# Channel attention with a SwiGLU stage on one core: low parts of split operands change engines, two differences become one, steps of the schedule move

## Chip, cores and metric

The kernel runs on one core of a Trainium2 chip. The metric is the device time of one execution in microseconds (us). Engines are called by their names: TensorE (PE in the profile; PEld is its weight load), VectorE (DVE), ScalarE (ACT), GpSimd (POOL), and SyncE (SP), whose queue issues most DMAs.

## The reference

```python
# attention over channels, per batch (B = 2, N = 6016 rows, C = 256 channels)
qn = q / (norm(q, axis=1) + 1e-6);  kn = k / (norm(k, axis=1) + 1e-6)
s = kn.transpose(0, 2, 1) @ qn / tau          # 256 x 256
a = softmax(s, axis=-1)
x = (v @ a).reshape(B * N, C)                 # 12032 x 256
# SwiGLU (d_ff = 1536)
xn = x / sqrt(mean(x * x, axis=-1) + 1e-6) * rms_g
g = xn @ w_gate;  val = xn @ w_val
out = (g * sigmoid(g) * val) @ w_out          # 12032 x 256
```

All is float32, and the output has 12032 rows of 256.

## The kernel before, in words

**Split operands.** Every matmul operand is kept as two fp32r tiles, a high part (the value rounded, made by ScalarE with a copy) and a low part (value minus high part, a subtraction). A product is three matmuls: high x high, high x low, low x high. Where the low parts are made, on VectorE or on GpSimd, is what much of the change is about.

**Blocks and steps.** The rows are worked on in 24 blocks of up to 512 rows (4 tiles of 128; the first of batch 0 and the last of batch 1 have 3). A block has 12 steps, f = 0 to 11, one for each 128 of the 1536 columns of w_gate and w_val. Blocks 0, 1 and 23 use plain products (`emit_hidden`). Blocks 2 to 22 use `emit_step`: seven products of half size in place of eight, for gate (even f) or value (odd f) of a pair p = f // 2. A step works on three flights at once: it starts f (products 5 and 1, into a PSUM tile pu of three buffers), continues f - 1 (3 and 6) and ends f - 2 (7, 2 and 4). ScalarE copies partial sums from PSUM into t (L810, L815), VectorE adds them to what comes later (L803, L804) into zg (gate) or zv (value). For a gate ScalarE applies SiLU (L819, L837); for a value VectorE multiplies it into zg (L822, and L831 for the quarter that product 4 ends). TensorE can't issue product 4 of a step before L803 has read its PSUM tile, nor use a tile again before L831 or L837 has. zg has two buffers, t two, zv one.

**Rounding and turned pairs.** After a pair's odd step `round_pair` lists its splits: gx (at the end of that step, `run_rounds` on ScalarE, then `run_subs` for the low part), gy and gz "later" (start of the next odd step). In blocks 4 to 22 the pairs 1 to 4 are turned: their output uses seven products too. gx is made of three quarters of zg (128x768). Then, in the middle of the next even step, `run_turned` overwrites the quarters of zg by differences, on VectorE, four of 128x256 (L728); gy (quarters 0 and 3) and gz (1 and 2) are split from these, the low parts on GpSimd (L742). As the low part of gx reads zg, the differences wait for it. In pairs 0 and 5 gx and gy have two quarters each (128x512) and nothing is overwritten. The output matmuls of f (L998) come five steps after f; a pair's first listed uses are of high parts.

**Order by hand.** The order on every engine is the order of emission. For blocks from 5 on, tables `steady_mid` (emitted in the middle of a step, after SiLU and differences or the product, ahead of the output matmuls) and `steady` (at the end of a step) say which step of the neighbouring blocks' work goes where. j is the block of the step:

- vm(0), v1: VectorE transposes (L427) of halves of v of block j + 3 or j + 2 into vw (one buffer); vh0, vh1: their high parts (ScalarE, L443); vl0, vl1: low parts (L448); x0, x1: px = v x a on TensorE (L459); q, r, n: squares (ScalarE, L475), reciprocal root (GpSimd, L484 and L488) and scaling (ScalarE, L500), into the tile "xn" of one buffer.
- m0, m1: VectorE transposes (L539) of the normalised rows of block j + 2 into a tile "moved" of one buffer; m1 also issues 16 DMAs of 32 KB on SP's queue (L548), which bring the turned rows into "xn".
- scale: ScalarE (L558) for block j + 1; parts: three GpSimd differences of xn's quarters (L570, L575), into "moved"; xh0, xh1 and xl0, xl1: high (L601) and low parts (L614) of the two rounds of xt of block j + 1, each round two operations (128x256 and 128x512; two of 128x512).
- copy, sums_, c0, c1 (VectorE, L1023, L1032): the output sums of block j - 1; store: two VectorE transposes (L1043) and four DMAs of 128 KB; load: four DMAs of 128 KB of v for block j + 3, into the buffer that store used.

In blocks 0 to 3 other tables hold; block 4 has `turn4` and `turn4_mid`, which override some entries. Before, vl0, vl1, xl0 and xl1 of the blocks from 4 on are on VectorE; xl1 is emitted in two parts (xl1a, xl1b).

Of the kernel before, what the change touches and what calls it, by code (L numbers as in the profile page):

```python
# [12 lines left out]
ALU = mybir.AluOpType  # L13
# [6 lines left out]
def kernel(  # L20
# [17 lines left out]
    nc = tc.nc  # L38
# [54 lines left out]
    def f32(ap):  # L93
        return ap.bitcast(F32)
# [61 lines left out]
    for b, sizes in enumerate(([2] * 2 + [4] * 9 + [2] * 3 + [1], [CH] * 11 + [3])):  # L156
        t = 0
# [174 lines left out]
    for b in range(B):  # L332
        t = 0
        while t < NT:
            n = (NT - t) % BT or BT if b == 0 else min(BT, NT - t)
# [6 lines left out]
    v_t, v_w, vT, xps, xnt, xT, xp, moved = {}, {}, {}, {}, {}, {}, {}, {}  # L342
# [36 lines left out]
    def half_tiles(j, h):  # L379
        return list(range(2 * h, min(2 * h + 2, blocks[j][2])))  # L380
# [61 lines left out]
        new_vT(j, h)  # L442
        nc.scalar.activation(out=vT[j, h][0][:, :, :m], in_=v_w[j, h][:, :, :m], func=AF.Copy)  # L443

    def split_v_low(j, h):
        m = len(half_tiles(j, h)) * P
        vh, vl = (x[:, :, :m] for x in vT[j, h])
        nc.vector.tensor_tensor(out=vl, in0=v_w.pop((j, h))[:, :, :m], in1=f32(vh), op=ALU.subtract)  # L448

    def emit_x(j, h):  # L450
        ah, al = a_hl[blocks[j][0]]
# [125 lines left out]
    def xT_round(j, i):  # L577

        h = blocks[j][2] * P // 2
        slots = ((0, 1), (1, 3)) if i == 0 else ((3, 5), (5, 7))  # L580
        hi, lo = ([y[:, a:b] for a, b in slots] for y in xp[j])
        if i == 0:
            whole = moved[j][0] if isinstance(moved[j], tuple) else moved[j]
            x = [whole[:, c, :2 * h].rearrange("p (i n) -> p i n", i=2) for c in range(KC)]
            src = [x[0][:, :1], x[1]]
        else:
            src = [moved[j][1][:, m:m + 2, :h] for m in (0, 2)]
        return src, hi, lo

    def emit_xT_high(j, i):  # L590
        if i == 0:
            new_xT(j)
        if j == NB - 1:
            if i == 0:
                nc.scalar.activation(
                    out=xT[j][0], in_=moved[j][:, :, :blocks[j][2] * P], func=AF.Copy
                )
            return
        src, hi, _ = xT_round(j, i)
        for o, x in zip(hi, src):  # L600
            nc.scalar.activation(out=o, in_=x, func=AF.Copy)  # L601

    def emit_xT_low(j, i, engine=nc.vector, part=None):
        if j == NB - 1:
            if i == 0:
                nc.vector.tensor_tensor(
                    out=xT[j][1], in0=moved[j][:, :, :blocks[j][2] * P], in1=f32(xT[j][0]),
                    op=ALU.subtract,
                )
            return  # L610
        src, hi, lo = xT_round(j, i)
        for k, (o, x, y) in enumerate(zip(lo, src, hi)):
            if part in (None, k):
                engine.tensor_tensor(out=o, in0=x, in1=f32(y), op=ALU.subtract)  # L614

    def emit_xT_round(j, i):
        emit_xT_high(j, i)
        emit_xT_low(j, i, nc.gpsimd)

# [60 lines left out]
    def so_part(tiles, m):  # L682
        if len(tiles) > 1 and m == 2:
            return tiles[1]
        return tiles[0][:, m * P:(m + 1) * P]
# [4 lines left out]
    rounds, subs, later, turned = [], [], [], []  # L690

    def new_g(tag, n, j, f):
        return [
            g_p.tile([P, n * HN], F32R, tag=f"{tag}{i}", name=f"g{tag}{i}_{j}_{f}") for i in range(2)
        ]

    def by_quarter(t, n, h):
        return t[:, :n * h].rearrange("p (i n) -> p i n", i=n)

    def round_pair(j, p, zg, h):  # L700

        x, y = new_g("x", 3, j, 2 * p), new_g("y", 2, j, 2 * p + 1)
        engine = nc.gpsimd
        w = [[w[:, 2 * p + i, e * P:(e + 1) * P] for w in wo] for i in range(2) for e in range(2)]
        if strassen(j, p):
            z = new_g("z", 2, j, 2 * p + 1)
            a12, a22, a11, s4 = w
            s1, s2, s3 = ([so_part(s[PAIRS.index(p)], m) for s in so_hl] for m in range(3))
            turned.append(zg)
            rounds.append((zg[:, :3], *(by_quarter(t, 3, h) for t in x), engine))  # L710
            later.append((zg[:, 0:4:3], *(by_quarter(t, 2, h) for t in y), engine))
            later.append((zg[:, 1:3], *(by_quarter(t, 2, h) for t in z), engine))
            q = [[t[:, i * h:(i + 1) * h] for t in x] for i in range(3)]
            r = [[t[:, i * h:(i + 1) * h] for t in g] for g in (y, z) for i in range(2)]
            G[j, 2 * p] = [(2, 0, a11, q[0]), (0, 0, a12, q[1]), (0, h, s4, q[2])]
            G[j, 2 * p + 1] = [
                (3, h, s1, r[0]), (3, 0, s3, r[1]), (1, 0, a22, r[2]), (2, h, s2, r[3]),
            ]
        else:
            rounds.append((zg[:, 1:3], *(by_quarter(t, 2, h) for t in x), engine))  # L720
            later.append((zg[:, 0:4:3], *(by_quarter(t, 2, h) for t in y), engine))
            for i, g in enumerate((x, y)):
                G[j, 2 * p + i] = [(e, 0, w[2 * i + e], [t[:, :2 * h] for t in g]) for e in range(2)]

    def run_turned():
        for z in turned:
            for o, i0, i1 in ((0, 3, 0), (3, 2, 3), (2, 2, 0), (1, 1, 2)):
                nc.vector.tensor_tensor(out=z[:, o], in0=z[:, i0], in1=z[:, i1], op=ALU.subtract)  # L728
        turned.clear()

    def strassen(j, p=PAIRS[0]):
        return STRA <= j < NB - 1 and p in PAIRS
# [6 lines left out]

    def run_subs():  # L740
        for hh, gh, gl, engine in subs:
            engine.tensor_tensor(out=gl, in0=hh, in1=f32(gh), op=ALU.subtract)  # L742
        subs.clear()

# [311 lines left out]
    with tc.manual_schedule():  # L1056
# [42 lines left out]
        for i in range(nch):  # L1099
            n = chunks[0][i][1]  # L1100
# [22 lines left out]
        parts = [(i, t, min(2, n - t)) for i, (_, n) in enumerate(chunks[1]) for t in range(0, n, 2)]  # L1123
# [70 lines left out]
        for f in range(NF):  # L1194
# [8 lines left out]
            n = 2 if f % 2 else 1  # L1203
# [31 lines left out]
        for i in (2, 3, 0, 1):  # L1235
            for p in range(NP):
                j, f = divmod(NF + at_step[p][i], NF)
# [8 lines left out]
        for p in range(NP):  # L1246
            j, f = divmod((NB - 2) * NF + 2 * p + 4, NF)
# [37 lines left out]
        def vm(h):  # L1285
            def run(n):
                move_v(n, h)
                if h == 1 and 2 < n + 1 < STRA + 2:
                    load_v(n + 1)
            return run  # L1290

        def vs(h):
            return lambda n: split_v(n, h)
# [13 lines left out]
        def xm(c):  # L1307
            return lambda n: emit_xT_move(n, c)
# [4 lines left out]
        def of(m, go):  # L1313

            def run(j):
                n = j + m
                if m < 0 and n < WINO or n >= NB:
                    return
                go(n)
            return run  # L1320

        v0, s0, v1, s1 = (of(2, go) for go in (vm(0), vs(0), vm(1), vs(1)))
        x0, q0, r0, n0, x1, q1, r1, n1 = (of(2, go(h)) for h in range(2) for go in (x, sq, rr, xn))
        m0, m1 = (of(2, xm(c)) for c in range(KC))
        scale, parts, hi, rest = (of(1, go) for go in (emit_xT_scale, emit_xT_parts, xr(0), xr(1)))
        copy, sums_, c0, c1, store = (of(-1, go) for go in (
            post_copy, post_sums, lambda j: post_out(j, 0), lambda j: post_out(j, 1), post_store,
        ))
        after = lambda m, *gos: tuple(of(m, go) for go in gos)
        load = of(3, load_v)  # L1330

        vh0, vl0, vh1, vl1 = (of(2, lambda n, go=go, h=h: go(n, h)) for h in range(2) for go in (split_v_high, split_v_low))
        xh0, xl0, xh1, xl1 = (of(1, lambda n, go=go, i=i: go(n, i)) for i in range(2) for go in (emit_xT_high, emit_xT_low))

        xl1a, xl1b = (of(1, lambda n, k=k: emit_xT_low(n, 1, part=k)) for k in range(2))

        steady = {
            0: (vl0,),
            1: (xh0, v1),
            2: (copy, sums_),  # L1340
            3: (vh1,),
            4: (c0, c1),
            5: (xh1,),
            7: (xl1b, load),
            8: (m0,),
            10: after(3, vm(0)),
        }
        steady_mid = {
            1: (scale,),
            2: (parts, xl0),  # L1350
            3: (x0, q0, r0),
            4: (vl1, n0),
            5: (x1, q1, r1),
            6: (n1, store),
            7: (xl1a,),
            9: (m1,),
            11: after(3, lambda n: split_v_high(n, 0)),
        }
        turn4 = {
            **steady,  # L1360
            0: (vh0,),
            1: (vl0,),
            2: (),
            3: (xh0, v1),
            4: (vh1, c0, c1),
        }
        turn4_mid = {
            **steady_mid,
# [1 line left out]
            2: (),  # L1370
            3: (scale,),
            4: (lambda j: build_so(2, 2), parts, xl0, x0),
            5: (vl1, q0, r0),
            6: (n0, x1, q1, r1, store),
            8: (n1,),
        }
        turn3 = {
            3: (v0,),
# [54 lines left out]
        for i, (j, f) in enumerate(steps):  # L1433
# [4 lines left out]
            k = min(j, 5)  # L1438
# [68 lines left out]
```

## Time and profile before

| what | value |
|---|---|
| time, median of 3 runs | 1349.29 us (1348.26 to 1349.37) |
| the profiled execution's own time | 1349.69 us |
| its span | 1347.7 us |
| mean granted TensorE clock | 0.996 |
| busy: TensorE / VectorE / ScalarE / GpSimd | 1272.7 / 1037.1 / 854.0 / 646.7 us |

Busy times are sums over the whole span, in which the first 200 us or so (scores, weights, the first two blocks) have other limits than the blocks from 4 to 22. Busy of TensorE includes the filling and draining of its pipeline, so a busy TensorE isn't one at its peak. A row of a timeline has the start in us, the duration (of all instructions of a merged row together), engine, line, operation, tiles and shapes, a count, and in brackets how long the engine stood before it and what ended that.

### The profile page before, as it was taken

How to read it: one execution, taken by the hardware profiler on the slowest of the kernel's cores; microseconds unless marked ns; L12 is line 12 of the kernel's file. 1: busy time of each engine (PE TensorE's matmuls, PEld its weight loads, DVE VectorE, ACT ScalarE, POOL GpSimd, SP SyncE). 2: the span in 40 equal slices, each digit the busy share in tenths (PEclk: the TensorE clock that was granted, in tenths of full speed). 3: DMA queues.
4: the chain of work that ended last, by engine and by line, in shares of the span. 5: the costliest groups of instructions: out<-in, count | busy, mean ns of one | idle time of the engine just before them, and what ended most of it. 6: DMA issues, size and time to landing. Idle time of an engine off the chain costs nothing.

```text
span 1347.7 us, 25377 instructions
## 1 busy us (share of the span) xinstructions
PE 1272.7 (94%) x9312; PEld 1205.9 (89%) x9312; DVE 1037.1 (77%) x1746; ACT 854.0 (63%) x1765; POOL 646.7 (48%) x531
## 2 busy tenths in 40 slices
PE   8999999998999899899999998998999999989998
PEld 7899889998889889898888898998988888989998
DVE  5799698677877877778788778777887887787763
ACT  5666557666666676666666676665666666766652
POOL 0210367465545545455455455455555554555550
PEclk9999999998999999999999999999999999999999
DMA  8966312022020220220211202202112012021021
GB/s 289 322 233 214 96 28 48 16 48 32 17 46 10 41 36 13 48 32 17 48 17 33 41 7 48 35 15 48 26 24 48 16 34 40 9 45 18 19 71 28
DMA packets 229372, 75.97 MB, mean 56 GB/s; under 512 B 186880, under 2 KB 220800, under 8 KB 229248
## 3 DMA queue, kind: packets, MB, share of 16 engines
q1 hardware_dynamic: 228416, 73.12, 22.9%
q8 instruction: 73, 1.20, 0.4%
q10 hardware_dynamic: 832, 1.25, 0.3%
q14 instruction: 51, 0.42, 0.1%
HBM read 48.50 MB, written 14.42 MB: 47 GB/s over the span
## 4 chain that ended last, share of the span: by engine, by line
PE 66%; DVE 15%; POOL 6%; DMA 4%; issue 4%; SPq 2%; ACT 2%; DVEq 0%; ACTq 0%; POOLq 0%
PE pu L774 30%; PE po L998 16%; POOL gx L742 6%; PE px L459 5%; DVE zg L728 4%; PE pq L774 4%; PE pg L891 3%; PE s L185 3%; PE pv L891 3%; PE po L944 3%; DVE zv L803 2%; DMA raw<-in_k_dram 2%; DVE vt L448 2%; SPq L548 2%; DVE xw L539 2%
## 5 line engine op out<-in xcount | busy, mean ns | idle before, releaser
L774 PE MATMUL pu<-xt,w 128*128 128x256 f32 x2268 | 397.6, 284 | 43.8 <-DVE zv L803 40.6
L774 PEld LDWEIGHTS pu<-xt,w 128*128 128x128 f32 x2268 | 326.7, 189 | 64.9 <-DVE zv L803 51.3
L774 PE MATMUL pu<-xt,s 128*128 128x256 f32 x2268 | 362.4, 284 | 18.9 <-DVE zg L831 17.7
L774 PEld LDWEIGHTS pu<-xt,s 128*128 128x128 f32 x2268 | 314.5, 189 | 35.2 <-DVE zg L831 24.7
L742 POOL TENSOR_TENSOR gx<-zg,gx 128x768 fp32r<-128x768 f32 (+1 forms) x126 | 205.6, 1632 | 216.3 <-PE pu L774 131.1
L742 POOL TENSOR_TENSOR gy<-zg,gy 128x512 fp32r<-128x512 f32 x126 | 165.8, 1316 | 227.1 <-ACT gy L736 214.1
L815 ACT ACTIVATE t<-pu 128x512 f32<-128x512 f32 x252 | 150.8, 598 | 147.3 <-DVE zv L804 105.8
L728 DVE TENSOR_TENSOR zg<-zg 128x256 f32<-128x256 f32 x304 | 129.3, 425 | 126.3 <-POOL gx L742 118.5
L998 PE MATMUL po<-gx,w 128*128 128x256 f32 (+1 forms) x984 | 190.0, 314 | 0.0
L822 DVE TENSOR_TENSOR zg<-zg,zv 128x768 f32<-128x768 f32 x126 | 161.7, 1283 | 12.4 <-DVE zv L804 0.9
L736 ACT ACTIVATE gx<-zg 128x768 fp32r<-128x768 f32 (+1 forms) x126 | 95.9, 761 | 113.4 <-DVE zg L831 103.0
L998 PEld LDWEIGHTS po<-gx,w 128*128 128x128 f32 x984 | 140.5, 188 | 4.7
L774 PE MATMUL pq<-xt,w 128*128 128x256 f32 x756 | 130.3, 281 | 0.0
L810 ACT ACTIVATE t<-pu 128x256 f32<-128x256 f32 x252 | 94.5, 375 | 38.8 <-PE pu L774 38.4
L742 POOL TENSOR_TENSOR gz<-zg,gz 128x512 fp32r<-128x512 f32 x76 | 111.5, 1467 | 0.0
L803 DVE TENSOR_TENSOR zg<-pu,t 128x512 f32<-128x512 f32 x126 | 85.3, 677 | 32.4 <-PE pu L774 22.5
L736 ACT ACTIVATE gy<-zg 128x512 fp32r<-128x512 f32 x126 | 80.5, 639 | 46.6 <-DVE zg L728 45.4
L774 PEld LDWEIGHTS pq<-xt,w 128*128 128x128 f32 x756 | 107.4, 190 | 0.0
L819 ACT ACTIVATE zg<-zg 128x768 f32<-128x768 f32 x126 | 105.9, 840 | 0.1
L803 DVE TENSOR_TENSOR zv<-pu,t 128x512 f32<-128x512 f32 x126 | 84.2, 669 | 15.9 <-ACT zg L837 7.6
L185 PE MATMUL s<-raw 128*128 128x256 f32 x376 | 86.2, 382 | 4.1 <-DMA raw<-in_k_dram 4.0
L998 PE MATMUL po<-gy,w 128*128 128x512 f32 x300 | 85.4, 393 | 0.0
(173 smaller groups left out, 2160.9 us busy)
## 6 DMA issues: line engine op xcount, KB each, us to landing
v<-in_v_dram SPq DMA_DIRECT2D x84, 128.0 KB, 3.7
xnT<-xw SPq DMA_DIRECT2D x336, 32.0 KB, 1.9
out_dram<-ob SPq DMA_DIRECT2D x84, 128.0 KB, 3.3
raw<-in_q_dram SPq DMA_DIRECT2D x20, 512.0 KB, 5.5
raw<-in_k_dram SPq DMA_DIRECT2D x19, 512.0 KB, 6.2
wraw<-in_moe_w_gate_dram SPq DMA_DIRECT2D x12, 256.0 KB, 5.7
wraw<-in_moe_w_val_dram SPq DMA_DIRECT2D x12, 256.0 KB, 5.9
wraw<-in_moe_w_out_dram SPq DMA_DIRECT2D x12, 256.0 KB, 5.6
```

The costliest lines, as they stand in the source:

```text
L185: nc.tensor.matmul(out=s_ps[b][:, c, :], lhsT=r[:, 1, t, c * P:(c + 1) * P], rhs=r[:, 0, t, :], start=(t0 + t == 0 and c == 0), stop=(t0 + ...
L728: nc.vector.tensor_tensor(out=z[:, o], in0=z[:, i0], in1=z[:, i1], op=ALU.subtract)
L736: nc.scalar.activation(out=gh, in_=hh, func=AF.Copy)
L742: engine.tensor_tensor(out=gl, in0=hh, in1=f32(gh), op=ALU.subtract)
L774: nc.tensor.matmul(out=out, lhsT=wm[wi], rhs=xm[xi], start=(start and q == 0), stop=(q == 2), skip_group_check=True,)
L803: nc.vector.tensor_tensor(out=z[:, 1:], in0=u, in1=t[:, :2], op=ALU.add)
L810: nc.scalar.activation(out=mt[:, 0], in_=mu[:, 1], func=AF.Copy)
L815: nc.scalar.activation(out=nt[:, 1:], in_=nu, func=AF.Copy)
L819: nc.scalar.activation(out=zg[:, 1:], in_=zg[:, 1:], func=AF.Silu)
L822: nc.vector.tensor_tensor(out=zg[:, 1:], in0=zg[:, 1:], in1=z, op=ALU.mult)
L891: nc.tensor.matmul(out=t[:, :n], lhsT=wgv[wi][:, f, c, wj, :], rhs=x[xi][:, c, :n], start=(m == 0), stop=(m == 3 * KC - 1),)
L998: nc.tensor.matmul(out=acc[b][:, o:o + g.shape[-1]], lhsT=w, rhs=g, start=first, stop=True, skip_group_check=True,)
```

## The change

In turned pairs the low part of gx is made by VectorE in `run_turned`, directly ahead of the differences; `run_subs` passes over it. The first two of the four differences become one instruction over quarters 0 and 3, with the quarters 3 and 2 in reversed order as first input. The low parts vl0, vl1, xl0 and xl1 go from VectorE to GpSimd. In the tables, v1 goes from the end of step 1 to the middle of step 2, xl0 from the middle of 2 to that of 3, q0 and r0 from 3 to 4, n0 from the middle of 4 to the end of 5, xh1 from the end of 5 to that of 4, xl1 from 7 to the end of 5, store from the middle of 6 to that of 5, m0 from the end of 8 to that of 6, m1 from the middle of 9 to the end of 8; block 4 has similar moves, among them n1 from the middle of 8 to that of 7.

```diff
-    def split_v_low(j, h):
+    def split_v_low(j, h, engine=nc.gpsimd):
...
-        nc.vector.tensor_tensor(out=vl, in0=v_w.pop((j, h))[:, :, :m], in1=f32(vh), op=ALU.subtract)
+        engine.tensor_tensor(out=vl, in0=v_w.pop((j, h))[:, :, :m], in1=f32(vh), op=ALU.subtract)
...
-    def emit_xT_low(j, i, engine=nc.vector, part=None):
+    def emit_xT_low(j, i, engine=nc.gpsimd):
...
-        for k, (o, x, y) in enumerate(zip(lo, src, hi)):
-            if part in (None, k):
-                engine.tensor_tensor(out=o, in0=x, in1=f32(y), op=ALU.subtract)
+        for o, x, y in zip(lo, src, hi):
+            engine.tensor_tensor(out=o, in0=x, in1=f32(y), op=ALU.subtract)
...
-            turned.append(zg)
-            rounds.append((zg[:, :3], *(by_quarter(t, 3, h) for t in x), engine))
+            rounds.append((zg[:, :3], *(by_quarter(t, 3, h) for t in x), None))
+            turned.append((zg, *(by_quarter(t, 3, h) for t in x)))
...
     def run_turned():
-        for z in turned:
-            for o, i0, i1 in ((0, 3, 0), (3, 2, 3), (2, 2, 0), (1, 1, 2)):
+        for z, gh, gl in turned:
+            nc.vector.tensor_tensor(out=gl, in0=z[:, :3], in1=f32(gh), op=ALU.subtract)
+            nc.vector.tensor_tensor(
+                out=z[:, 0:4:3], in0=z[:, 3:1:-1], in1=z[:, 0:4:3], op=ALU.subtract
+            )
+            for o, i0, i1 in ((2, 2, 0), (1, 1, 2)):
                 nc.vector.tensor_tensor(out=z[:, o], in0=z[:, i0], in1=z[:, i1], op=ALU.subtract)
...
         for hh, gh, gl, engine in subs:
+            if engine is None:
+                continue
...
         steady = {
             0: (vl0,),
-            1: (xh0, v1),
+            1: (xh0,),
             2: (copy, sums_),
             3: (vh1,),
-            4: (c0, c1),
-            5: (xh1,),
-            7: (xl1b, load),
-            8: (m0,),
+            4: (xh1, c0, c1),
+            5: (xl1, n0),
+            6: (m0,),
+            7: (load,),
+            8: (m1,),
             10: after(3, vm(0)),
         }
         steady_mid = {
             1: (scale,),
-            2: (parts, xl0),
-            3: (x0, q0, r0),
-            4: (vl1, n0),
-            5: (x1, q1, r1),
-            6: (n1, store),
-            7: (xl1a,),
-            9: (m1,),
+            2: (parts, v1),
+            3: (xl0, x0),
+            4: (vl1, q0, r0),
+            5: (x1, q1, r1, store),
+            6: (n1,),
             11: after(3, lambda n: split_v_high(n, 0)),
         }
         turn4 = {
             **steady,
-            0: (vh0,),
-            1: (vl0,),
+            0: (vh0, vl0),
...
+            5: (xh1, xl1),
+            6: (),
+            7: (m0, load),
         }
         turn4_mid = {
...
-            5: (vl1, q0, r0),
-            6: (n0, x1, q1, r1, store),
-            8: (n1,),
+            5: (vl1, q0, r0, store),
+            6: (n0, x1, q1, r1),
+            7: (n1,),
         }
```

## Rows read from the trace of the kernel before

**Rows 1.** The page, busy time of each engine.

```profile
PE 1272.7 (94%) x9312; PEld 1205.9 (89%) x9312; DVE 1037.1 (77%) x1746; ACT 854.0 (63%) x1765; POOL 646.7 (48%) x531
```

**Rows 2.** The table of waits: who waited for whom, us in total, times, longest.

```profile
DVE zg L728 <- POOL gx L742: 118.5, 74, 2.0
...
PE pu L774 <- DVE zv L803: 40.6, 50, 1.6
```

**Rows 3.** Windows of a block's length: us, busy time of each engine, granted clock.

```profile
313.00:366.00 53.00, 46.52 (x340) 45.05 (x339) 44.27 (x73) 31.66 (x73) 29.59 (x22) 0.90 0.17 31
366.00:419.00 53.00, 49.35 (x385) 47.26 (x384) 40.60 (x72) 33.67 (x72) 28.20 (x23) 1.00 0.17 31
1162.00:1215.00 53.00, 49.46 (x386) 47.35 (x385) 41.28 (x73) 34.23 (x73) 28.09 (x24) 1.00 0.16 29
1215.00:1268.00 53.00, 51.99 (x404) 49.65 (x403) 39.62 (x74) 34.58 (x71) 28.50 (x23) 1.00 0.12 23
```

**Rows 4.** The chain of waits, 875 to 930 us: start, us, what.

```profile
894.75 1.41 PE pu L774 x12
...
897.57 0.70 PE po L998 x3
```

**Rows 5.** Timeline of VectorE, 875 to 930 us.

```profile
876.63 1.80 DVE L728 TENSOR_TENSOR zg<-zg 128x256 f32<-128x256 f32 x4 [1.99 <-POOL gx L742]
...
884.91 1.80 DVE L728 TENSOR_TENSOR zg<-zg 128x256 f32<-128x256 f32 x4 [1.99 <-POOL gx L742]
886.63 1.80 DVE L448 TENSOR_TENSOR vt<-vw,vt 128x512 fp32r<-128x512 f32 x1
...
892.27 2.92 DVE L614 TENSOR_TENSOR xt<-xnT,xt 128x256 fp32r<-128x256 f32 x2
...
900.74 1.32 DVE L448 TENSOR_TENSOR vt<-vw,vt 128x512 fp32r<-128x512 f32 x1
...
907.86 0.43 DVE L831 TENSOR_TENSOR zg<-pu,zg 128x256 f32<-128x256 f32 x1 [1.30 <-PE pu L774]
...
909.54 0.41 DVE L804 TENSOR_TENSOR zg<-pq,t 128x256 f32<-128x256 f32 x1
...
920.81 1.81 DVE L728 TENSOR_TENSOR zg<-zg 128x256 f32<-128x256 f32 x4 [1.39 <-POOL gx L742]
...
929.71 0.43 DVE L728 TENSOR_TENSOR zg<-zg 128x256 f32<-128x256 f32 x1 [2.00 <-POOL gx L742]
```

**Rows 6.** Timeline of TensorE, 875 to 930 us.

```profile
879.74 0.62 PE L774 MATMUL pu<-xt,w 128*128 128x256 f32 x3 [0.54 <-DVE zv L803]
...
889.08 0.62 PE L774 MATMUL pu<-xt,w 128*128 128x256 f32 x3 [1.57 <-DVE zv L803]
...
914.85 0.62 PE L774 MATMUL pu<-xt,w 128*128 128x256 f32 x3
...
917.94 0.62 PE L774 MATMUL pu<-xt,s 128*128 128x256 f32 x3 [0.58 <-DVE zg L831]
...
926.84 0.62 PE L774 MATMUL pu<-xt,s 128*128 128x256 f32 x3 [0.46 <-DVE zg L831]
```

**Rows 7.** Timeline of ScalarE, 875 to 930 us.

```profile
882.11 0.85 ACT L736 ACTIVATE gx<-zg 128x768 fp32r<-128x768 f32 x1 [0.85 <-DVE zg L831]
```

**Rows 8.** Instructions of lines 822 and 614: duration in ns, min/median/max.

```profile
L822 DVE TENSOR_TENSOR zg<-zg,zv x126: 957/1266/1873, 207.6 to 1303.9; 128x768 f32<-128x768 f32 x126
...
L614 DVE TENSOR_TENSOR xt<-xp,xt x36: 674/676/1778, 324.1 to 1235.4; 128x512 fp32r<-128x512 f32 x36
```

**Rows 9.** Timeline of GpSimd, 875 to 930 us.

```profile
886.59 1.29 POOL L742 TENSOR_TENSOR gy<-zg,gy 128x512 fp32r<-128x512 f32 x1 [1.72 <-ACT gy L736]
887.84 1.72 POOL L742 TENSOR_TENSOR gz<-zg,gz 128x512 fp32r<-128x512 f32 x1
...
907.97 0.71 POOL L488 TENSOR_TENSOR rr<-ss,mhalf 128x2 f32<-128x2 f32 x1
```

**Rows 10.** Timeline of TensorE, 300 to 372 us (block 4).

```profile
329.93 1.23 PE L998 MATMUL po<-gy,so 128*128 128x256 f32 x4 [2.73 <-ACT xn L500]
```

More of the change, by code (lines that the diff above doesn't have):

```diff
@@ L601, in emit_xT_high @@
             nc.scalar.activation(out=o, in_=x, func=AF.Copy)
-    def emit_xT_low(j, i, engine=nc.vector, part=None):
+    def emit_xT_low(j, i, engine=nc.gpsimd):
         if j == NB - 1:
             if i == 0:
-                nc.vector.tensor_tensor(
+                engine.tensor_tensor(
                     out=xT[j][1], in0=moved[j][:, :, :blocks[j][2] * P], in1=f32(xT[j][0]),
@@ L611, in emit_xT_low @@
         src, hi, lo = xT_round(j, i)
-        for k, (o, x, y) in enumerate(zip(lo, src, hi)):
-            if part in (None, k):
-                engine.tensor_tensor(out=o, in0=x, in1=f32(y), op=ALU.subtract)
+        for o, x, y in zip(lo, src, hi):
+            engine.tensor_tensor(out=o, in0=x, in1=f32(y), op=ALU.subtract)
     def emit_xT_round(j, i):
         emit_xT_high(j, i)
-        emit_xT_low(j, i, nc.gpsimd)
+        emit_xT_low(j, i)
     s_hl = []
@@ L1333 @@
         xh0, xl0, xh1, xl1 = (of(1, lambda n, go=go, i=i: go(n, i)) for i in range(2) for go in (emit_xT_high, emit_xT_low))
-        xl1a, xl1b = (of(1, lambda n, k=k: emit_xT_low(n, 1, part=k)) for k in range(2))
         steady = {
             0: (vl0,),
-            1: (xh0, v1),
+            1: (xh0,),
             2: (copy, sums_),
             3: (vh1,),
-            4: (c0, c1),
-            5: (xh1,),
-            7: (xl1b, load),
-            8: (m0,),
+            4: (xh1, c0, c1),
[3 more added lines that the diff above has]
+            8: (m1,),
             10: after(3, vm(0)),
```

## The prediction

> **What bounds the kernel now.** I read the page first: TensorE is busy for 94% of the span [rows 1], so what can be won is TensorE's idle time and what each stop costs beyond it. The table of waits says who causes it: TensorE's largest wait is for VectorE's sum into zv, and VectorE's own largest wait is, 74 times, for GpSimd's low part of gx ahead of the differences of a turned pair [rows 2]. Next the windows of one block's length: the 16 from 366 to 1215 us have 3.6 us of idle TensorE each on average (first and last shown), the window ahead of them 6.5 us at a granted clock of 0.90, the one behind them only 1.0 us [rows 3].
>
> What a stop costs is seen in the chain of waits and on TensorE's line. Undisturbed, twelve matmuls of 256 columns take 1.41 us, 0.1178 us each, and three of 512 columns 0.70 us [rows 4]. A block from 5 to 20 issues 252 + 84 + 24 = 360 of the first kind (products, outputs of the four turned pairs, px) and 24 of the second (pairs 0 and 5): 360 x 0.1178 + 8 x 0.70 = 48.0 us. Its period is 53.08 us, between the same differences one block apart (876.63 and 929.71) [rows 5]. So a block loses 5.05 us. On TensorE's line that is five stops a block with 3.63 us of idle in all (first, last and two between shown); the rest, (5.05 - 3.63) / 5 = 0.28 us a stop, is draining and restarting, which the profile counts as busy.
>
> The longest stop shows the mechanism. The ScalarE rounding of gx ends at 882.96 us [rows 7]. VectorE has been free since 882.92, but stands 1.99 us until GpSimd has made the low part, because the differences overwrite what GpSimd reads; four differences then take 1.80 us, and the low part of v, in the same step, another 1.80 us to 888.43 [rows 5]. Only then come the zv sums, which TensorE awaits at 889.08 after 1.57 us of idle [rows 6].
>
> **The change, part by part.**
>
> Low part of gx to VectorE, 76 times. It loses the waits: four a block, 6.6 us together (first 1.99, last 1.39) [rows 5]. It adds a subtraction of 128x768 from two SBUF tensors to an fp32r tile. The same shape, with an f32 result, is the product of line 822, 0.957 us at least, 1.873 at most [rows 8]. I take 0.96, because GpSimd has nothing else at that moment; 1.87 is the bad end. A block pays 4 x 0.96 = 3.8 us. It now waits for the ScalarE rounding, and behind it on VectorE stand the differences, transposes and zv sums; in the step above the rounding ended 0.04 us after VectorE was free, so I cost that at nothing. The cover is the zg sums (about 1.0 us), without them the 0.85 us of the rounding would be paid.
>
> Two differences as one: 128x512 instead of two of 0.45 us start to start [rows 5]. No row has a reversed input. Between 0.60 (dense, 0.674 for 128x512 less overlap [rows 8]) and 0.90 (no gain) I take 0.68, the dense row's time; 0.9 us less a block.
>
> Low parts of v and x to GpSimd. VectorE loses, in a block, 1.80 and 1.32 for v, 2.92 for the two of the first round of x [rows 5] and 2 x 0.68 for the second [rows 8]: 7.4 us. GpSimd gains six operations, 1.29 us for each of 128x512 as in the row of gy [rows 9], less for the one of 128x256, and loses four of gx at some 1.95 (882.96 to 884.91 [rows 5, 7]); its load is nearly unchanged. Three VectorE or ScalarE steps now wait for GpSimd, since their tiles have one buffer: v1 for vl0, q0 for xl0, m0 for xl1. Behind m0 on VectorE stand the zv sums, for which TensorE waits; v1 and q0 come more than a step after GpSimd can have ended.
>
> Moves. The transposes of store go behind the product of step 5; there VectorE idles 1.30 us until TensorE delivers (L831 at 907.86) [rows 5], so their 1.3 us cost nothing. If that slack goes, L831 is late by it. The store's four DMAs, the four loads of v and the 32 KB moves of x stay in their order on SP's queue, the stores and the moves one step earlier, the loads where they were: nothing, with three steps or more until the transposes and scales that need them. v1 goes to the middle of step 2, where xl0's 2.92 us leave VectorE. q0 and r0 go one step back, n0 more than one: covered, since the first px's PSUM is wanted only in step 7. xh1 goes one step ahead, behind the parts that GpSimd makes in step 2. In block 4, n1 comes a step earlier: there TensorE stood 2.73 us for it [rows 10].
>
> Retiming the longest stop: low part 882.96 to 883.92, differences to 885.4, no low part of v, zv sums to about 886.1. TensorE would have gone on at the latest at 889.08 - 1.57 = 887.51 and, without the drain, some 0.2 us earlier. The stop goes, with 1.2 us to spare. The other stops lie behind the same waits, behind transposes or the second low parts of x, and lack 0.46 to 0.58 us [rows 6] where the step gains 1 us or more. What is late next is step 6: its GpSimd work for rr ends at 908.68, then two low parts of x run to 911.3, while VectorE is ready for gx's at 909.95 [rows 5, 9]. Taking turns (below), VectorE makes gx's until 910.96, GpSimd holds it until 912.25, then differences, m0's transposes and the first zv sum follow to about 915.0, where TensorE went on at 914.85 [rows 6].
>
> **The lock.** The low part of v, 0.674 us undisturbed for its shape, took 1.80: it began at 886.63, 0.04 us behind a GpSimd subtraction that ended at 887.88, and needed 0.55 more; GpSimd's next then took 1.72 instead of 1.29 [rows 5, 8, 9]. So such operations take turns, and a moved operation holds VectorE for up to 1.29 us. In step 6 that is the turn priced above: 0.15 us late at the first sum, some 0.2 more at the product, and a restart, 0.65 us a block. (The Trainium skill, SBUF — State Buffer, section "Who interferes with whom", states this as an exclusive lock between a VectorE instruction with two SBUF inputs and a GpSimd one that reads SBUF, the loser blocked for the whole instruction; the trace agrees with the 1.80 us. GPSIMD Engine Reference, section 4.1, would keep elementwise sums on VectorE. By these two, six longer holds a block speak against the change; the sum with a collision each is the first rival's.)
>
> The sum: 16 blocks x 5.05 = 81; block 4 and its surroundings 6.5 of idle, four restarts 1.1 and about 3.5 for the low clock (between 0 and 0.10 x 53 = 5.3) = 11; block 21 about 2 [rows 3]: 94 us. Against this 17 x 0.65 = 11 for step 6 and 3 left in block 4. 1349.7 (the profiled execution: span 1347.7 and 2.0 around it, 0.4 above the median of the runs) - 94 + 14 = 1269.7; against the median 1269.3. I say 1270.
>
> **The rivals.**
>
> 1. *GpSimd's turns keep part of the stops.* The buffers of zg are two, so a cycle closes: zg sums 0.60 + 0.41, low part 0.96, differences of gy 0.68, rounding 0.63, GpSimd gy 1.29, VectorE's product taking its turn 0.96, GpSimd gz 1.29: 6.8 us. TensorE's pair takes 63 x 0.1178 = 7.42 us. One more turn of 1.29 gives 8.1: 0.7 a pair, 2.8 a block and with step 6 3.4, so 17 x 1.6 + 9 = 36 us of gain, 1313 us. For it: the margin is only 0.6 us. Against: the moved operations lie mostly in steps 0 to 5, without differences. Chance 0.19.
> 2. *Slower: two turns in every turned pair.* If gz and one moved operation both fall ahead of the differences, the cycle is 6.8 + 2.6 = 9.4 us, 8.0 a block instead of 5.05: 1349 + 17 x 2.9 = 1398 us. It decides from 8.7 us a cycle, where the pair stands now (7.42 + 5.05 / 4). Against: GpSimd stays below 30 us of work in 53 [rows 3]. Chance 0.08.
> 3. *No change: the stops are handed on.* The second px then waits for the low part of v, now behind gx's and x's in GpSimd's queue, for the 5 us: 1349. Against: by the rows' durations it is done over 2 us ahead of px. Chance 0.05.
>
> **How the numbers follow.** My forecast has 0.68. Its own range is 1256 (every stop gone, 1349.7 - 94) to 1290 (low part of gx at 1.87 us in half the pairs, reversed input without gain). About 0.03 may lie beneath it. The range of 8 in 10 takes in the first rival's centre: 1256 to 1313. About 0.2% is what a measurement of this kernel tells from no change; faster has 0.68 + 0.19, less 0.01 for a first rival grown worse: 0.86; same 0.05, slower 0.09.
>
> **What would show it.** In the new profile: no wait of L728 for GpSimd's gx; the new low part at 0.96 us, at most some at 1.9; the joined difference below 0.75; TensorE idle below 1 us in a block's window; a period near 48.7 us; what remains standing in steps 6 to 8, behind L614 on GpSimd; no half-clock window in block 4. The forecast is wrong if the period stays above 50 us, if the waits of VectorE for GpSimd (zg sums for gz, low part for x) exceed 2 us a block, or if TensorE waits for px's low part.

## The result, and the profile after

The changed kernel takes 1268.19 us (median of 4 runs, 1266.93 to 1270.91) where the kernel before takes 1348.78 us in the same comparison: a ratio of 0.9406, 95% interval 0.9389 to 0.9423. The forecast was 1270. The profiled execution took 1268.32 us with a span of 1266.5, so 81.4 us less than the one before.

First the page's row of busy times, which answers to [rows 1]:

```profile
PE 1251.8 (99%) x9312; PEld 1198.9 (95%) x9312; DVE 1004.8 (79%) x1637; ACT 859.7 (68%) x1767; POOL 671.8 (53%) x564
```

TensorE has gone from 94% to 99% of the span. VectorE's busy time is only 32 us less, so it wasn't relieved of much work; it waits less. Two ScalarE instructions are new (1767, before 1765): they come back below.

Windows of a block's length (us, busy time of each engine, granted clock), which answer to [rows 3]: block 4 and two steady ones.

```profile
300.00:348.50 48.50, 44.21 (x325) 41.75 (x324) 39.46 (x68) 32.91 (x74) 26.38 (x22) 0.96 0.20 37
348.50:397.00 48.50, 48.50 (x388) 47.21 (x387) 40.87 (x68) 35.27 (x75) 30.18 (x25) 1.00 0.19 34
...
1027.50:1076.00 48.50, 48.50 (x388) 47.21 (x387) 39.81 (x67) 34.76 (x74) 30.17 (x25) 1.00 0.19 34
```

Where 3.6 us of idle stood, none is left. Next VectorE's timeline. The first two rows are the store's transposes of neighbouring blocks; then step 0, which answers to the longest stop of before; then steps 6 and 7.

```profile
1000.35 1.30 DVE L1048 STREAM_TRANSPOSE ob<-os 128x512 f32<-128x512 f32 x2
1048.73 1.30 DVE L1048 STREAM_TRANSPOSE ob<-os 128x512 f32<-128x512 f32 x2
...
833.46 0.96 DVE L726 TENSOR_TENSOR gx<-zg,gx 128x768 fp32r<-128x768 f32 x1
834.46 0.69 DVE L727 TENSOR_TENSOR zg<-zg 128x512 f32<-128x512 f32 x1
835.18 0.89 DVE L731 TENSOR_TENSOR zg<-zg 128x256 f32<-128x256 f32 x2
836.15 0.69 DVE L808 TENSOR_TENSOR zv<-pu,t 128x512 f32<-128x512 f32 x1
...
858.94 0.95 DVE L726 TENSOR_TENSOR gx<-zg,gx 128x768 fp32r<-128x768 f32 x1
859.92 1.67 DVE L727 TENSOR_TENSOR zg<-zg 128x512 f32<-128x512 f32 x1
...
864.21 1.81 DVE L827 TENSOR_TENSOR zg<-zg,zv 128x768 f32<-128x768 f32 x1
```

The period is 48.38 us (1048.73 - 1000.35), before 53.08. In step 0, VectorE goes from gx's low part through the differences to the zv sums in 2.7 us without standing. In step 6 the joined difference takes 1.67 us instead of 0.69, the turn that the forecast placed there. GpSimd's side of it, two low parts of x together:

```profile
857.72 3.32 POOL L613 TENSOR_TENSOR xt<-xp,xt 128x512 fp32r<-128x512 f32 x2
```

Undisturbed, as in the run below that moves them, the two take 2.55 us. VectorE's low part of gx got in between them, and the second held up the joined difference. All 15 of the 76 joined differences that take 1.67 us lie in step 6. What TensorE loses is seen a step later (its timeline; the first row shows six matmuls with nothing late):

```profile
862.27 0.87 PE L779 MATMUL pu<-xt,s 128*128 128x256 f32 x6
...
863.91 0.61 PE L779 MATMUL pu<-xt,w 128*128 128x256 f32 x3
...
865.88 1.14 PE L779 MATMUL pu<-xt,s 128*128 128x256 f32 x6
```

Three matmuls take 0.52 and six 0.87 where nothing is late, so 0.09 us go at the first sum and 0.27 behind VectorE's product in step 7 (1.81 us above, in a turn with gz), about 0.36 us a block.

Block 4 has a stop that wasn't there before (timelines of ScalarE, then of TensorE):

```profile
298.06 0.40 ACT L601 ACTIVATE xt<-xnT 128x256 fp32r<-128x256 f32 x1
303.05 0.63 ACT L601 ACTIVATE xt<-xnT 128x512 fp32r<-128x512 f32 x1 [4.58 <-DMA xnT<-xw]
```

```profile
304.61 0.63 PE L779 MATMUL pu<-xt,s 128*128 128x256 f32 x3 [2.85 <-ACT t L815]
```

The new table `turn4` takes over the entries of `steady`, and no longer has one of its own for step 1. So xh0 is emitted there, ahead of the scaling, and again in step 3. That is the two instructions more, and ScalarE waits 4.58 us for moves of x that nobody needs yet. Behind TensorE's stop the granted clock falls to the lower of its two levels for 3.4 us (0.64 on average from 304 to 308 us).

### The profile page after: what moved, and what is told of

Read it like the earlier page. It is cut to its first block, busy times and chain, and to the rows that moved or that the text cites. A ratio compares the mean times of both kernels' runs of the same rounds, so it can differ in the third digit from the quotient of the medians.

```text
span 1266.5 us, 25188 instructions
## 1 busy us (share of the span) xinstructions
PE 1251.8 (99%) x9312; PEld 1198.9 (95%) x9312; DVE 1004.8 (79%) x1637; ACT 859.7 (68%) x1767; POOL 671.8 (53%) x564
## 4 chain that ended last, share of the span: by engine, by line
PE 87%; DVE 4%; DMA 3%; ACT 2%; SPq 1%; issue 1%; POOL 1%; ACTq 0%; DVEq 0%; POOLq 0%
PE pu L779 39%; PE po L1003 23%; PE pq L779 6%; PE px L459 5%; PE s L185 5%; PE pg L896 3%; PE pv L896 3%; PE po L949 3%; DMA raw<-in_k_dram 2%; SPq L548 1%; SPq L353 0%; DVE gx L726 0%; DVE zg L808 0%; POOL gz L747 0%; DVE zg L727 0%
## 5 line engine op out<-in xcount | busy, mean ns | idle before, releaser
L779 PE MATMUL pu<-xt,w 128*128 128x256 f32 x2268 | 391.9, 281 | 1.6 <-DVE zg L808 1.3
L779 PE MATMUL pu<-xt,s 128*128 128x256 f32 x2268 | 355.5, 282 | 4.5 <-ACT t L815 2.8
L747 POOL TENSOR_TENSOR gy<-zg,gy 128x512 fp32r<-128x512 f32 x126 | 176.9, 1404 | 313.9 <-ACT gy L739 294.3
L827 DVE TENSOR_TENSOR zg<-zg,zv 128x768 f32<-128x768 f32 x126 | 169.2, 1343 | 11.3 <-DVE zv L809 0.5
L747 POOL TENSOR_TENSOR gz<-zg,gz 128x512 fp32r<-128x512 f32 x76 | 116.4, 1532 | 0.0
L747 POOL TENSOR_TENSOR gx<-zg,gx 128x512 fp32r<-128x512 f32 x50 | 65.2, 1304 | 41.1 <-ACT gx L739 40.9
L185 PEld LDWEIGHTS s<-raw 128*128 128x128 f32 x376 | 70.2, 191 | 14.4 <-DMA raw<-in_k_dram 3.2
```

What stands on the lines that cost most here:

```text
L185: nc.tensor.matmul(out=s_ps[b][:, c, :], lhsT=r[:, 1, t, c * P:(c + 1) * P], rhs=r[:, 0, t, :], start=(t0 + t == 0 and c == 0), stop=(t0 + ...
L779: nc.tensor.matmul(out=out, lhsT=wm[wi], rhs=xm[xi], start=(start and q == 0), stop=(q == 2), skip_group_check=True,)
L827: nc.vector.tensor_tensor(out=zg[:, 1:], in0=zg[:, 1:], in1=z, op=ALU.mult)
```

## The experiments

In all of them the time of before lay between 1347.78 and 1348.58 us (medians of the runs beside them).

### gx's low part back on GpSimd

```diff
-            rounds.append((zg[:, :3], *(by_quarter(t, 3, h) for t in x), None))
+            rounds.append((zg[:, :3], *(by_quarter(t, 3, h) for t in x), engine))
...
     def run_turned():
         for z, gh, gl in turned:
-            nc.vector.tensor_tensor(out=gl, in0=z[:, :3], in1=f32(gh), op=ALU.subtract)
```

> The changed kernel with one part undone: gx's low part in turned pairs on GpSimd again, all else as changed. My theory (a turned pair's chain from ScalarE's rounding of gx to the zv sums stops TensorE): the differences end 1.87 - 0.96 = 0.9 us later in each pair, and the cycle of the two zg buffers becomes 1.0 + 1.87 + 0.69 + 0.63 + 1.3 + 0.96 + 1.3 = 7.8 us against TensorE's 7.42: 1.4 us a block, and in step 6 the low parts of x come behind gx on GpSimd, some 1 us more: 1268 + 17 x 2.4 = 1309 us, between 1290 and 1325, with VectorE waiting for GpSimd's gx again. Rival (the gain comes from taking the low parts of v and x off VectorE, and where gx's is made matters little): within 3 us of 1268.

Measured: 1338.98 us, ratio 0.9925 (0.9910 to 0.9940). The rival falls, but the price is 71 us, beyond my range. Step 6 has the longest stop, seen in the timelines of VectorE, GpSimd and TensorE:

```profile
800.49 1.77 DVE L726 TENSOR_TENSOR zg<-zg 128x512 f32<-128x512 f32 x1 [1.24 <-POOL gx L746]
802.29 2.82 DVE L730 TENSOR_TENSOR zg<-zg 128x256 f32<-128x256 f32 x2
```

```profile
798.62 1.84 POOL L746 TENSOR_TENSOR gx<-zg,gx 128x768 fp32r<-128x768 f32 x1 [0.64 <-ACT gx L738]
800.41 3.00 POOL L613 TENSOR_TENSOR xt<-xp,xt 128x512 fp32r<-128x512 f32 x2
803.38 1.45 POOL L746 TENSOR_TENSOR gy<-zg,gy 128x512 fp32r<-128x512 f32 x1
```

```profile
806.37 0.62 PE L778 MATMUL pu<-xt,w 128*128 128x256 f32 x3 [2.07 <-DVE zv L807]
```

With gx ahead of them in the queue, both low parts of x and then gy fall among the three differences: 4.6 us instead of 1.6. Shorter stops, of 0.3 us and in some blocks 0.7 us, lie elsewhere. The mean granted clock is 0.988 here, with eight stretches of 3.4 to 6.8 us at the lower level, but that isn't the price: from 533 to 1215 us the periods with such a stretch last 52.4 to 52.9 us, those without 52.3 to 52.4, so all five of them together cost about 1 us.

### The low parts of v and x back on VectorE

```diff
-    def split_v_low(j, h, engine=nc.gpsimd):
+    def split_v_low(j, h, engine=nc.vector):
...
-    def emit_xT_low(j, i, engine=nc.gpsimd):
+    def emit_xT_low(j, i, engine=nc.vector):
...
-        emit_xT_low(j, i)
+        emit_xT_low(j, i, nc.gpsimd)
```

> The changed kernel with one part undone: the low parts of v and x of the steady blocks on VectorE again, at the changed places in the steps. My theory: the chain of a turned pair has over 1 us to spare in most steps, so what returns to VectorE costs only where it stands ahead of zv or zg sums: vl0 in step 0 (0.68 to 1.8 us, spare 1.2) and xl1 at the end of step 5 (1.4 us, spare 0.65): up to 1 us a block, 1270 to 1285 us. Rival (VectorE's total work is the bound, 7.4 us more in a block): 1268 + 17 x 4 = 1336 us or more, near the time before.

Measured: 1265.54 us, ratio 0.9384 (0.9370 to 0.9398): not slower at all. Both theories expected a loss. VectorE's timeline has the low part of v in step 0, and the store's transposes for the period; the row of GpSimd's gy follows:

```profile
834.71 0.68 DVE L448 TENSOR_TENSOR vt<-vw,vt 128x512 fp32r<-128x512 f32 x1
...
998.38 1.30 DVE L1048 STREAM_TRANSPOSE ob<-os 128x512 f32<-128x512 f32 x2
1046.42 1.30 DVE L1048 STREAM_TRANSPOSE ob<-os 128x512 f32<-128x512 f32 x2
```

```profile
834.96 1.59 POOL L747 TENSOR_TENSOR gy<-zg,gy 128x512 fp32r<-128x512 f32 x1 [4.89 <-ACT gy L739]
```

The instruction that took 1.80 us before [rows 5] takes 0.68 in 15 of 16 blocks (1.80 in the other). GpSimd still works beside it, but the order has turned: before, VectorE started 0.04 us behind gy; now it starts 0.16 to 0.26 us ahead, and gy waits (1.59 us here instead of 1.29). The period is 48.04 us: what TensorE needs by itself (the forecast had counted 48.0).

### gx's low part alone, in the old order

The kernel before with the new `run_turned` and `run_subs`; tables, and the engines of the low parts of v and x, as before.

> The kernel before with one part of the change alone: gx's low part on VectorE and two differences as one, the order of steps and the low parts of v and x as before. My theory: the differences end 1.3 us earlier in each turned pair; of the five stops those of 0.54, 0.48, 0.46 and 0.58 us go or nearly go, the one of 1.57 us keeps about 0.4 because vl0 still follows: a block loses 1 to 2 us instead of 5.05, 1349 - 17 x 3.5 = 1290 us, between 1275 and 1305. Rival (both parts are needed, since VectorE's load stays with 3.8 us more in a block): above 1320 us.

Measured: 1289.90 us, ratio 0.9564 (0.9550 to 0.9579), on the forecast. Two stops are left in every block (TensorE):

```profile
829.27 0.62 PE L780 MATMUL pu<-xt,s 128*128 128x256 f32 x3 [0.53 <-DVE zg L837]
...
837.48 0.62 PE L780 MATMUL pu<-xt,s 128*128 128x256 f32 x3 [0.48 <-DVE zg L837]
```

They lie behind xl1a (1.77 us in a turn with gz) and behind the transposes of m1, which follow a product of 1.61 us. The new order takes xl1 and m1 out of these places. The longest stop of before, behind vl0, is left in 2 of 16 blocks only, those in which GpSimd's gy starts ahead of vl0 (1.79 and 1.81 us); in the other 14 vl0 starts 0.15 to 0.18 us ahead of gy and takes 0.68 us. From block 5 on, its place in step 0 is the same in the old order and the new.

### The old order with the new engines

The changed kernel with both pairs of tables of before, xl1 again in two parts.

> The changed kernel with the order of steps of before (both tables of the steady blocks and of block 4), engines as changed: gx's low part on VectorE, low parts of v and x on GpSimd. My theory: the moves are worth little by themselves, since what VectorE and TensorE wait for is gone by the change of engines. With the old order xl1 stands on GpSimd in step 7 beside gy and gz, which costs at most one turn of 1.3 us a block against a slack near 0.6, and block 4 gets back its stop of 2.7 us but loses the early xh0 (4.6 us of waiting for a move of x): 1262 to 1290 us. Rival (the new order carries the gain): above 1300 us.

Measured: 1283.62 us, ratio 0.9517 (0.9501 to 0.9533): within the range, with two stops of 0.4 us left in most blocks (TensorE), behind the transposes of m0 and m1:

```profile
829.11 0.62 PE L780 MATMUL pu<-xt,w 128*128 128x256 f32 x3 [0.39 <-DVE zv L809]
...
832.02 0.62 PE L780 MATMUL pu<-xt,s 128*128 128x256 f32 x3 [0.41 <-DVE zg L837]
```

### The new order alone

The first two undoings together: gx's low part on GpSimd, those of v and x on VectorE; only the order and the joined difference are new.

> The changed order of steps and the joined difference alone: gx's low part on GpSimd, the low parts of v and x on VectorE, as before. In the runs so far the order of steps was worth 24 us where gx's low part was on VectorE. My theory (the order takes extras out of the steps that wait for gx, so it helps there too): 1310 to 1328 us. Rival (without gx's low part on VectorE every turned step still waits, and the order is worth nothing): 1345 us or more.

Measured: 1298.37 us, ratio 0.9636 (0.9621 to 0.9650), 12 us below my range. One stop a block stays, the one of step 0 (VectorE, then TensorE):

```profile
804.03 0.69 DVE L726 TENSOR_TENSOR zg<-zg 128x512 f32<-128x512 f32 x1 [1.99 <-POOL gx L746]
...
805.57 1.78 DVE L448 TENSOR_TENSOR vt<-vw,vt 128x512 fp32r<-128x512 f32 x1
```

```profile
808.00 0.62 PE L778 MATMUL pu<-xt,w 128*128 128x256 f32 x3 [1.36 <-DVE zv L807]
```

VectorE still stands 1.99 us for gx in this pair; where no low part of v follows, that reaches TensorE no more.

### Four differences again

```diff
-            nc.vector.tensor_tensor(
-                out=z[:, 0:4:3], in0=z[:, 3:1:-1], in1=z[:, 0:4:3], op=ALU.subtract
-            )
-            for o, i0, i1 in ((2, 2, 0), (1, 1, 2)):
+            for o, i0, i1 in ((0, 3, 0), (3, 2, 3), (2, 2, 0), (1, 1, 2)):
```

> The changed kernel with one part undone: four differences of 128x256 in a turned pair instead of one of 128x512 and two. The trace of the changed kernel has the joined one at 0.69 us, two single ones at 0.85 to 0.89: 0.2 us more a pair, in a chain with 1 us to spare in three of the four pairs, and in step 6 one more instruction that can fall into GpSimd's turn. My theory: 1268 to 1272 us. Rival (the chain has no slack left): 17 x 4 x 0.2 = 14 us more, 1282 us.

Measured: 1270.24 us, ratio 0.9419 (0.9406 to 0.9432), not to be told from the changed kernel.

### Block 4 without the second xh0

```diff
             0: (vh0, vl0),
+            1: (),
             2: (),
```

> The changed kernel without the second emission of xh0 in block 4. The changed table of block 4 no longer overrides step 1 of the steady one, so ScalarE makes the high parts of the first round of x already there, ahead of the rows' scaling, and again in step 3. In the trace it waits 4.6 us for the moves of x, TensorE then stands 2.85 us and runs some us at half clock. My theory: 2.9 + 0.3 for the restart + about 1.3 for the clock = 4.5 us less, 1263 to 1265 us. Rival (the stop only moves to the next wait in block 4): 1267 to 1268 us.

Measured: 1263.05 us, ratio 0.9368 (0.9355 to 0.9381): 5.1 us below the changed kernel, as expected.

### The same, with xl1 ahead of the second root

```diff
-            5: (xl1, n0),
+            5: (n0,),
...
-            5: (x1, q1, r1, store),
+            5: (xl1, x1, q1, r1, store),
```

> As the run without the second xh0, and the low parts of the second round of x ahead of the second reciprocal root in GpSimd's queue (emitted first in the middle of step 5, no longer at its end). The block's period is 48.38 us in the changed kernel, 48.03 in the run with these low parts on VectorE, which I take for TensorE's own time. My theory (the 0.36 us a block come from GpSimd's turn ahead of the differences in step 6): the turn falls into step 5, beside the store's transposes, the period becomes 48.03 to 48.1 and the time 17 x 0.36 = 6 us less than in the run without the second xh0: 1256 to 1260 us. Rival (the work of the second root, now later, makes m0 or the squares late): no less than that run, 1263 us or more.

Measured: 1258.26 us, ratio 0.9330 (0.9317 to 0.9343), 4.8 us below the run without the second xh0, and the fastest version of all. VectorE in step 6, and the period:

```profile
947.44 0.95 DVE L726 TENSOR_TENSOR gx<-zg,gx 128x768 fp32r<-128x768 f32 x1
948.42 0.69 DVE L727 TENSOR_TENSOR zg<-zg 128x512 f32<-128x512 f32 x1
...
950.65 0.71 DVE L539 STREAM_TRANSPOSE xw<-xn 128x512 f32<-128x512 f32 x1 [0.62 <-ACT xn L500]
...
991.77 1.30 DVE L1048 STREAM_TRANSPOSE ob<-os 128x512 f32<-128x512 f32 x2
1039.81 1.30 DVE L1048 STREAM_TRANSPOSE ob<-os 128x512 f32<-128x512 f32 x2
```

One joined difference of 76 still takes 1.67 us, and the period is 48.04 us. The later root does make m0's transposes late, by 0.62 us, which the turn no longer taken pays for.

### Low parts on VectorE, without the second xh0

The same line in `turn4` as above.

> As the run with the low parts of v and x on VectorE, without the second xh0 in block 4. My theory: the same 4.5 us as from the changed kernel: 1265.5 - 4.5 = 1261 us, between 1259 and 1263, with the period of 48.03 us unchanged. Rival (block 4 has another bound here, with more of VectorE's work in it): less than 2 us gained, 1264 us or more.

Measured: 1266.85 us, ratio 0.9394 (0.9379 to 0.9408): nothing gained, the rival was right. VectorE and TensorE in block 4:

```profile
295.52 0.69 DVE L448 TENSOR_TENSOR vt<-vw,vt 128x512 fp32r<-128x512 f32 x1 [2.40 <-ACT vt L443]
```

```profile
300.41 0.63 PE L779 MATMUL pu<-xt,w 128*128 128x256 f32 x3 [2.57 <-DVE zv L808]
```

With vl0 on VectorE behind vh0 of the same step, VectorE stands 2.40 us, then still has the output weights to prepare, and TensorE stops 2.57 us with or without the second xh0, whose wait was hidden beside it. The traced execution had 3.4 us at the lower clock behind this stop (0.5 from 302 to 305 us), which that of the run above hadn't; one of the four executions had a mean granted clock of 1.000, and took 1264.53 us.

### gz's low part twice

```diff
-            later.append((zg[:, 1:3], *(by_quarter(t, 2, h) for t in z), engine))
+            later.append((zg[:, 1:3], *(by_quarter(t, 2, h) for t in z), "twice"))
...
-            engine.tensor_tensor(out=gl, in0=hh, in1=f32(gh), op=ALU.subtract)
+            n = 2 if engine == "twice" else 1
+            engine = nc.gpsimd if engine == "twice" else engine
+            for _ in range(n):
+                engine.tensor_tensor(out=gl, in0=hh, in1=f32(gh), op=ALU.subtract)
```

> The changed kernel with one cost doubled: GpSimd makes gz's low part twice in every turned pair (the second writes the same values). This tests the cycle of the first rival, which the two buffers of zg close. My theory: the cycle (zg sums 1.0, gx's low part 0.96, joined difference 0.69, rounding 0.63, gy 1.3, VectorE's product in its turn 0.96, gz 1.3 = 6.8 us) becomes 8.1 us against TensorE's 7.42, 0.7 us in each of four pairs; about 1 us of spare time is used up first in each block: 1.8 us a block (1.5 to 2.8), 1268 + 17 x 1.8 = 1299 us, between 1290 and 1316, and the zg sums wait for GpSimd. Rival (the pairs follow TensorE alone and GpSimd has room): under 1273 us.

Measured: 1310.43 us, ratio 0.9728 (0.9712 to 0.9744); the period is 50.26 us, 1.88 more than in the changed kernel, where 1.8 was expected. The whole is 42 us slower, not the 31 forecast: the 16 steady periods account for 32, the blocks ahead of and behind them for the rest. The cycle is seen on VectorE's line, one turned pair apart:

```profile
840.72 0.69 DVE L811 TENSOR_TENSOR zg<-pu,t 128x512 f32<-128x512 f32 x1 [0.84 <-POOL gz L750]
...
848.65 0.69 DVE L811 TENSOR_TENSOR zg<-pu,t 128x512 f32<-128x512 f32 x1 [0.85 <-POOL gz L750]
```

7.93 us a pair, the first rival's 8.1 but for 0.2, against TensorE's 7.42.

### A fill in place of the second gz

gz's entry is marked as in the run above; here the mark brings a fill.

```diff
+            if engine == "twice":
+                engine = nc.gpsimd
+                engine.memset(f32(gl), 0.0)
             engine.tensor_tensor(out=gl, in0=hh, in1=f32(gh), op=ALU.subtract)
```

> As the run with gz's low part twice, but the added GpSimd operation is a fill of gz's low tile with zeros ahead of its low part: it writes and reads nothing in SBUF. It lies at the same place of the cycle. My theory (two-input operations take turns with GpSimd's only where GpSimd reads): it adds its own duration alone, by the fills in the trace under 0.8 us for 128x512, and VectorE's product doesn't wait for it: the cycle stays at 7.4 to 7.6 us and the time below 1285 us. Rival (any GpSimd operation takes such a turn): as the run with gz twice, or its share by duration of more than half.

Measured: 1264.59 us, ratio 0.9383 (0.9369 to 0.9397), its interval overlapping that of the changed kernel. GpSimd and VectorE in step 7:

```profile
860.32 1.30 POOL L750 TENSOR_TENSOR gy<-zg,gy 128x512 fp32r<-128x512 f32 x1 [1.60 <-ACT gy L739]
861.55 0.53 POOL L749 MEMSET gz<- 128x512 f32 x1
862.17 1.83 POOL L750 TENSOR_TENSOR gz<-zg,gz 128x512 fp32r<-128x512 f32 x1
```

```profile
861.89 0.96 DVE L830 TENSOR_TENSOR zg<-zg,zv 128x768 f32<-128x768 f32 x1
```

VectorE's product starts while the fill runs and takes its undisturbed 0.96 us; gz then waits for it. From 400 to 1180 us these products have a mean of 0.99 us, in the changed kernel 1.37. So not every operation on GpSimd holds VectorE: the subtraction, which reads two tiles in SBUF, did, and the fill, which reads none, didn't. (One that reads a single tile wasn't tried.) In step 6 the joined difference takes 1.67 us in 15 of 76 cases as before, but the period is 48.11 us, so 0.27 us of the changed kernel's 0.36 come from the turn of the product in step 7.

## Why the prediction was right, point by point

**The bound and what a stop costs** held. TensorE by itself needs 48.04 us a block, in three kernels (low parts on VectorE, with and without the second xh0, and xl1 first); the forecast counted 48.0. Sixteen periods, store to store, went from 850.1 to 776.5 us: 73.6 us, where 16 x (5.05 - 0.65) = 70 was forecast. The remaining 7.8 us lie in block 4 and at the ends, where 10 was forecast net.

**gx's low part** took 0.96 us (median 0.958 of 76, mean 0.983), the joined difference 0.69 undisturbed, and VectorE's wait of 118.5 us for GpSimd's gx is gone. Undoing this part gives back 71 of the 80 us.

**Step 6** was the right place for what remains, by the right mechanism, but mis-sized: 0.36 us a block, not 0.65. The delays were 0.09 us at the first sum and 0.27 at the product, where 0.15 and 0.2 were forecast; what wasn't paid is the restart of 0.28. Moving xl1 away removed both.

**The cycle of the first rival** is real, as the doubled gz shows. It didn't decide in the changed kernel: in the pairs of steps 8, 10 and 0 the joined difference took 0.69 us throughout, so no further turn fell there.

**Two steps failed**, though the sum didn't show it. First, "VectorE loses 7.4 us" by the low parts of v and x. The 1.80, 2.92 and 1.32 us were mostly turns behind GpSimd, not work. In the new order with gx's low part on VectorE the low parts of v cost 0.68 to 0.75 us there in nearly all blocks, all six of a block 4.0 us in place of 7.5, and the place where they are made is worth next to nothing. The four kernels with the new order and the joined difference, all with the second xh0 (us):

| | low parts of v, x on VectorE | on GpSimd |
|---|---|---|
| gx's low part on GpSimd | 1298.37 | 1338.98 |
| gx's low part on VectorE | 1265.54 | 1268.19 |

GpSimd can't take both: 41 us are lost in the upper row, nothing is won in the lower; without the second xh0 the lower row is 1266.85 and 1263.05, 3.8 us for GpSimd. Second, "moves: nothing". They were costed for what they might break, not for what they bring. The order took 24 us off with the low parts on VectorE (1289.90 to 1265.54), 15 with them on GpSimd (1283.62 to 1268.19), and 49 with neither on its new engine (1347.78 to 1298.37, the joined difference included). My sum gave all five stops to the engines; two of them would have stayed, as the run with the new engines in the old order shows (0.39 and 0.41 us, period 49.34 us).

So it is in part luck that the forecast was off by no more than 2 us. The new engines in the old order take 1283.62 us, some 14 above the forecast, and the moves, put at nothing, made up for it. In step 6 the sum took off 0.29 us a block too much, 5 us over 17 blocks, which about balances the second xh0.

**Block 4**: I read the table of differences and not the merged table, and so missed that xh0 is now emitted twice, 5.1 us. The 3 us that I had left standing there for other reasons hid part of it. The sign that block 4 would have no half-clock window failed too (0.64 from 304 to 308 us); without the second xh0 the granted clock is 1.00 from 300 to 356 us.

## What to carry to other kernels

A long instruction in a trace may be a short one in a queue for something shared: compare it with the shortest of its shape before you count its time as work that a move would save. Where two remedies act on the same stop, their gains don't add, so undo them one by one before you say which of them paid. And when a table is built from another by overriding, read the merged one.

## What the runs showed of the hardware that I had not expected

The turns have an order that a small shift decides. The low part of v in step 0 started 0.04 us behind GpSimd's gy in the kernel before and took 1.80 us; with gx's low part alone moved it started some 0.16 us ahead in 14 of 16 blocks and took 0.68, while gy took 1.67 instead of 1.29. VectorE's product in step 7 took 1.81 us in the changed kernel, where gz started ahead of it, and 0.96 with a fill of 0.53 us between gy and gz. More GpSimd work made the period shorter there (48.11 instead of 48.38 us).

A reversed input costs a VectorE subtraction next to nothing: 0.691 us for 128x512 (median), against 0.676 for the dense one of line 614 [rows 8].
